# Attention and two feed-forward layers on one core: token blocks by batch, with the short tails gathered in the last block

## The chip, the cores and the metric

The kernel runs on one core of a Trainium2 chip. The metric is the device time of one execution in microseconds (us). Before the change it is 985.03 us, the median of three runs (984.52 to 985.04). Everything is computed in one launch; the host only rearranges inputs.

The engines are named as the profile names them: PE is TensorE (PEld its weight loads), DVE is VectorE, ACT is ScalarE, POOL is GpSimd, SP is SyncE, which issues most of the DMAs.

## The reference

Four batches of 8 heads, 576 queries and keys each, head size 64; then 2304 tokens of width 512 go through two feed-forward layers:

```
scores = q k^T / 8, plus min(-(cum[query] - cum[key]), 0), causal mask
attn   = softmax(scores);   x = attn v                 # [4 * 576, 8 * 64] = [2304, 512]
x      = ((x w_a) * (x w_b)) w_out                     # inner width 1536
h      = x w_in;  g = max(h, 0) + alpha * min(h, 0)    # inner width 2048
out    = g w_out2
```

`cum` is the running sum of max(s, 0) along a head's 576 positions.

## The kernel before

**Tokens.** PE works on blocks of tokens: three of 512 and a last one of 768 (`sizes`, L417). A block is a stretch of 512 or 768 *consecutive* tokens of the 2304, so its borders do not fall on those of the batches, which have 576 tokens. Block 1, for example, holds the last 64 tokens of batch 0 and the first 448 of batch 1. The inputs of the feed-forward layers lie in `xh` and `xl` (two buffers each, 512 tokens, used by the blocks in turn) and, for what is over, in `ovh` and `ovl` (256 tokens). Each number is held as a rounded part (`h`) and a rest (`l`), and each product is made of three matmuls (`mm3`, L1247).

**Attention.** A batch's 576 queries are worked on in two parts: the first 512 (four row tiles of 128, r = 0 to 3), and the last 64, which the text calls the *tail* of the batch (r = 4). For a pair of heads `hp` (four pairs to a batch) the steps are: `loads` (queries and keys `kq`, running sums `cb`, values `v`), `biases` (the bias and mask into a tile `z`), the scores (`s01`, `s23` for the first 512; `s4` for the tail), softmax on DVE and ACT (`soften`), a turn of the probabilities by DVE blocks (`zt`) and through DRAM (`zd`, then read back into `pt` or, for the tail, into the single buffer `pb`), and the product with the values (`av` for the first 512, `av_b` for the tail; `two_av` does both, the tail's first). What leaves `av` is split into `xh` and `xl`; `pieces` (L421) says which part of it goes to which block's tiles, so that the product of batch 1 is split in two pieces (448 and 64 tokens) and that of batch 2 too (384 and 128).

**What runs when.** Batch 0's first 512 queries are done before any feed-forward work (`first_attention`). The rest is a list of steps for each block (`plan`, made by `attention`), which PE takes up between the matmuls of that block: while block 0 is computed, the tail of batch 0 and the first 512 of batch 1; while block 1 is, the tail of batch 1 and the first 512 of batch 2; while block 2 is, the tail of batch 2, batch 3's first 512, and batch 3's tail. A list may begin with a `lead`, put at the end of the list before it (L1919); that of block 0 is issued within `first_attention`, as are its first six steps. Empty steps (`SPACE`) keep a distance before the last product; in block 2 five of them are filled with the first steps of the tail of batch 3, and the other 14 stand behind (L1900).

**What sets the order.** The order of all instructions on each engine is written out when the kernel is built. PE's order follows the loops; that of DVE, ACT, POOL and SP comes from a small model of the engines (`Order`), in which each chain of operations asks for an engine, and the one that could start first gets it; some operations choose between two engines there. `due` takes the next step when its share of the block is reached; `possible` (L1259) may put off scores and `two_av` until their inputs are there by the model; for `av_b` alone it does not look. Each engine then executes its list in order: an instruction that waits holds all behind it.

**Last block.** Block 3 (`ffn_seven`) has no attention beside it. It needs the first 512 tokens and all 256 in `ovh` and `ovl`. At its end `out_2` makes six tiles of 128 tokens of the result, and `store` and `leave` send each to DRAM with one DMA. At the start of blocks 1 and 2 the tokens in `ovh` and `ovl` are copied into the next block's `xh` and `xl` (L1921 to L1924).

Of the kernel before, what the change touches and what calls it, by code (L numbers as in the profile page):

```python
# [21 lines left out]
P = 128  # L22
# [189 lines left out]
def attention_two_moe_kernel(  # L212
# [10 lines left out]
    nc = tc.nc  # L223
# [194 lines left out]
    blocks = [(sum(sizes[:i]), n) for i, n in enumerate(sizes)]  # L418
    NB = len(blocks)

    def pieces(t0, n, blk):  # L421

        b0 = blocks[blk][0]
        k = max(0, min(n, b0 + 512 - t0))
        if k:
            yield 0, k, xh[blk % 2], xl[blk % 2], t0 - b0
        if k < n:
            yield k, n - k, ovh, ovl, t0 + k - b0 - 512
# [357 lines left out]
    def av(b, hp, blk):  # L786
# [25 lines left out]
        run.pe(4 * 1280 / 2.4)  # L812
        run.give(of_vb)
        x_done[blk].append(read_by(at, finish(pv, b * S, QA, hp, blk)))

    def finish(pv, t0, n, hp, blk):
        for o, k, dh, dl, c in pieces(t0, n, blk):
            yield from split(pv[:, o:o + k], dh[:, hp, c:c + k], dl[:, hp, c:c + k], False)
# [28 lines left out]
    def av_b(b, hp, blk):  # L847
# [18 lines left out]
        for c in range(0 if turned else 5):  # L866
# [9 lines left out]
        x_done[min(blk, NB - 1)].append(  # L876
            read_by(at, finish(pv, b * S + QA, QB, hp, min(blk, NB - 1)))
        )

    def two_av(a, b, hp, blk):  # L880

        av_b(b, hp, blk)
        av(a, hp, blk)
# [3 lines left out]
    def first_attention():  # L887
# [12 lines left out]
        for i in range(HP + 2):  # L900
# [8 lines left out]
            if 0 <= i - 2:  # L909
                av(0, i - 2, 0)  # L910
# [21 lines left out]
    def attention(blk):  # L932

        b, a = blk - 1, blk
        has_a = a < B
# [18 lines left out]
        if has_a:  # L954
            lead.append((both, (a, 0, (0, 1))))
        if not has_a or a >= TURN:
            lead.append((biases, (b, 0, (4,))))
        for i in range(HP + 1):
            j = i - 1

            def turns(c):
                for k in range(2 if a < TURN else 0):
                    add(turn, j, a, 2 * j + k, c)

            def last(p, k):
                if blk < TURN:
                    add(t4, p, b, p, k)

            if has_a and a >= TURN:
                add(s4, i, b, i)  # L970
                add(s01, i, a, i)
                add(loads, i + 1, i + 1)
                if blk > 1:
                    add(biases, i + 1, b, i + 1, (4,))
# [7 lines left out]
                if blk == 1:  # L982
                    add(biases, i + 1, b, i + 1, (4,))
                add(both, i + 1, a, i + 1, (0, 1))
            elif has_a:
                add(s01, i, a, i)
                add(both, i, a, i, (2,))
                turns(0)
                add(both, i, a, i, (3,))
                add(s23, i, a, i, 2)  # L990
                last(j, 0)
                turns(1)
                last(j, 1)
                add(s23, i, a, i, 3)
                add(biases, i, b, i, (4,))
                add(loads, i + 1, i + 1)
                turns(2)
                add(both, i + 1, a, i + 1, (0, 1))
                add(two_av, j, a, b, j, blk)
                add(s4, i, b, i)  # L1000
            else:
                add(loads, i + 1, i + 1)
                add(s4, i, b, i)
                add(biases, i + 1, b, i + 1, (4,))
                last(i, 0)
                last(i, 1)
                if i == HP:
                    steps.extend([(lambda: None, ())] * TAIL)
                add(av_b, i - (blk >= TURN), b, i - (blk >= TURN), blk)
# [249 lines left out]
    def possible(f, args):  # L1259
# [5 lines left out]
        if f == two_av:  # L1265
            a, b, hp, _ = args
# [33 lines left out]
    H2 = blocks[-1][1] // 2  # L1300
# [143 lines left out]
    def ffn_seven(blk, sums):  # L1444
        t0, T = blocks[blk]
# [227 lines left out]
        def leave(t, o):  # L1673
            yield from dma(out[t0 + t * P:t0 + (t + 1) * P, :], o)
            run.give(of_t, run.t)

        def store(t):
# [3 lines left out]
            run.spawn(leave(t, o), run.t)  # L1681
# [44 lines left out]
        def out_2(f):  # L1726
# [4 lines left out]
            for t in range(T // P):  # L1731
# [8 lines left out]
                if t == T // P - 1:  # L1740
# [41 lines left out]
    def ffn(blk):  # L1782
        t0, T = blocks[blk]
# [56 lines left out]
        def store(t):  # L1840
# [3 lines left out]
            run.spawn(leave(t, o), run.t)  # L1844

        def leave(t, o):
            yield from dma(out[t0 + t * P:t0 + (t + 1) * P, :], o)
            run.give(of_t, run.t)
# [60 lines left out]
    for blk in range(NB):  # L1909
# [5 lines left out]
        T = blocks[blk][1]  # L1915
# [79 lines left out]
```

## Time and profile before

| | us |
|---|---|
| median of three runs | 985.03 |
| the profiled execution: span from first to last instruction | 982.3 |
| PE busy in it | 963.1 (98%) |
| DVE busy | 748.5 (76%) |
| ACT busy | 558.7 (57%) |
| POOL busy | 223.7 (23%) |
| median less span | 2.7 |

The page gives the profiled execution no time but its span; what the runs have over it, 2.7 us, is taken to lie around it. The page shows PE busy in nine tenths or more of every slice of a fortieth of the span except the first two. The matmuls are pipelined, so a busy PE need not be at its peak: beside the share, the waits of PE are to be read, and how far apart matmuls start.

By the lines of the trace, block 0's matmuls begin at 58 us, block 1's at 276, block 2's at 489 and block 3's at 709.

### The profile page before, as it was taken

What the parts mean: (1) busy time and instruction counts of PE and PEld (TensorE: products, weight loads), DVE (VectorE), ACT (ScalarE), POOL (GpSimd) and SP (SyncE); (2) the same over time, 40 slices, a digit from 0 to 9 for tenths busy, and PEclk for the clock granted to TensorE, in tenths of its full rate; (3) what the DMA queues carried; (4) which work ended last, traced back from release to release, by engine and by line L of the source; (5) the groups of instructions that cost most, each with busy time, mean ns of one, the idle gap of its engine ahead of it and who ended that gap; (6) DMA issues with size and microseconds to landing.
All of it is one profiled execution on the core that took longest, in us unless ns stands there. A gap on an engine that the chain in (4) does not pass through costs nothing.

```text
span 982.3 us, 15862 instructions
## 1 busy us (share of the span) xinstructions
PE 963.1 (98%) x5235; PEld 810.3 (82%) x5235; DVE 748.5 (76%) x1743; ACT 558.7 (57%) x1173; POOL 223.7 (23%) x290
## 2 busy tenths in 40 slices
PE   6989999999999999999999999999999999999998
PEld 5557787778888878888888888888899999999997
DVE  7777886986878788888478868666497888787782
ACT  6856675775855555665455547544552333476453
POOL 2131110431124234563135434522100000000000
PEclk9999999999999999999999999999999999999999
DMA  7589999899788979688388785855402212112101
GB/s 181 185 262 320 347 332 322 293 323 329 245 271 259 304 245 312 194 257 293 112 270 260 218 264 194 251 172 183 165 22 94 78 66 87 43 47 82 61 5 65
DMA packets 140083, 196.78 MB, mean 200 GB/s; under 512 B 35744, under 2 KB 79776, under 8 KB 140000
## 3 DMA queue, kind: packets, MB, share of 16 engines
q1 hardware_dynamic: 130208, 177.93, 58.0%
q10 hardware_dynamic: 9792, 17.83, 4.9%
q8 instruction: 41, 0.67, 0.3%
q14 instruction: 42, 0.34, 0.1%
HBM read 152.13 MB, written 43.59 MB: 199 GB/s over the span
## 4 chain that ended last, share of the span: by engine, by line
PE 84%; DMA 8%; DVE 5%; issue 1%; ACT 1%; SPq 0%; POOL 0%; ACTq 0%; DVEq 0%
PE bank L1248 18%; PE bank L1249 18%; PE bank L1250 18%; PE bank L1886 5%; PE bank L1888 4%; PE bank L1887 4%; DMA cb<-cum_d 3%; PE bank L1735 2%; PE bank L1734 2%; PE bank L1736 2%; PE bank L801 2%; DMA raw<-in_w_dram 2%; PE bank L563 2%; PE bank L544 1%; PE bank L741 1%
## 5 line engine op out<-in xcount | busy, mean ns | idle before, releaser
L1248 PE MATMUL bank<-xh,wh 128*128 128x512 f32 (+1 forms) x620 | 237.9, 384 | 2.0 <-DVE g L292 2.0
L1250 PE MATMUL bank<-xh,wl 128*128 128x512 f32 (+1 forms) x620 | 234.0, 377 | 0.0
L1249 PE MATMUL bank<-xl,wh 128*128 128x512 f32 (+1 forms) x620 | 234.0, 377 | 0.0
L284 ACT ACTIVATE wh<-raw 128x512 fp32r<-128x512 f32 (+1 forms) x198 | 115.1, 592 | 84.4 <-PE bank L1249 35.0
L1248 PEld LDWEIGHTS bank<-xh,wh 128*128 128x128 f32 x620 | 116.4, 188 | 26.1 <-issue 4.6
L1250 PEld LDWEIGHTS bank<-xh,wl 128*128 128x128 f32 x620 | 116.4, 188 | 19.3
L1249 PEld LDWEIGHTS bank<-xl,wh 128*128 128x128 f32 x620 | 116.4, 188 | 18.6
L301 POOL TENSOR_TENSOR wl<-raw,wh 128x512 fp32r<-128x512 f32 x69 | 91.5, 1329 | 110.9 <-ACT wh L284 71.1
L301 DVE TENSOR_TENSOR wl<-raw,wh 128x512 fp32r<-128x512 f32 (+1 forms) x135 | 84.6, 640 | 33.7 <-ACT wh L284 27.8
L276 ACT ACTIVATE z<-z,mn 128x512 f32<-128x512 f32 (+4 forms) x144 | 82.8, 577 | 47.3 <-DVE mn L292 45.9
L1248 PE MATMUL bank<-gh,wh 128*128 128x512 f32 (+1 forms) x240 | 89.5, 373 | 0.0
L1249 PE MATMUL bank<-gl,wh 128*128 128x512 f32 (+1 forms) x240 | 88.7, 370 | 0.4 <-DVE gl L301 0.2
L1250 PE MATMUL bank<-gh,wl 128*128 128x512 f32 (+1 forms) x240 | 88.5, 369 | 0.0
L284 ACT ACTIVATE gh<-g 128x512 fp32r<-128x512 f32 x84 | 52.8, 629 | 43.5 <-DVE g L292 40.1
L1886 PE MATMUL bank<-wh,gh 128*128 128x512 f32 x192 | 76.4, 398 | 0.0
L1029 ACT ACTIVATE top<-raw 128x512 f16<-128x512 bf16 x90 | 68.5, 784 | 12.3 <-DMA raw<-in_w_dram 10.9
L1888 PE MATMUL bank<-wh,gl 128*128 128x512 f32 x192 | 74.8, 389 | 0.0
L1887 PE MATMUL bank<-wl,gh 128*128 128x512 f32 x192 | 74.8, 389 | 0.0
L301 DVE TENSOR_TENSOR gl<-g,gh 128x512 fp32r<-128x512 f32 x69 | 51.6, 748 | 18.8 <-ACT gh L284 18.0
L292 DVE STREAM_TRANSPOSE zt<-z 128x384 f32<-128x384 f32 (+2 forms) x88 | 55.7, 648 | 2.4 <-DMA zd<-zt 1.4
L616 POOL TENSOR_SCALAR_AFFINE_SELECT z<-z 64x64 f32<-64x64 f32 (+2 forms) x80 | 34.0, 432 | 97.3 <-DVE z L606 63.7
L311 DVE TENSOR_SCALAR z<-z,sm 128x512 f32<-128x512 f32 (+4 forms) x100 | 55.0, 573 | 1.3
(151 smaller groups left out, 1918.1 us busy)
## 6 DMA issues: line engine op xcount, KB each, us to landing
raw<-w_d SPq DMA_DIRECT2D x91, 512.0 KB, 4.3
raw<-in_w_dram SPq DMA_DIRECT2D x90, 512.0 KB, 5.6
w_d<-w ACTq DMA_DIRECT2D x46, 256.0 KB, 5.0
zd<-zt SPq DMA_DIRECT2D x48, 192.0 KB, 5.0
pt<-zd SPq DMA_DIRECT2D x48, 192.0 KB, 4.9
kq<-in_kq_a_dram SPq DMA_DIRECT2D x16, 512.0 KB, 5.7
vb<-in_v_dram SPq DMA_DIRECT2D x112, 64.0 KB, 4.4
zd<-zt SPq DMA_DIRECT2D x24, 256.0 KB, 4.0
```

The lines of the kernel that those rows point to most:

```text
L276: nc.scalar.activation(o, i, func, **k)
L284: nc.scalar.activation(o, i, AF.Copy, scale=by)
L292: f(*args, **k)
L301: (nc.gpsimd if eng == "pool" else nc.vector).tensor_tensor(o, i0, i1, op=ALU.subtract)
L311: (nc.gpsimd if eng == "pool" else nc.vector).tensor_scalar(o, i, s0, s1, op0=ALU.mult, op1=ALU.mult)
L1029: nc.scalar.activation(top.bitcast(F16).rearrange("p (n t) -> p n t", t=2)[:, :, 1], r.bitcast(BF16)[:, 4:4 + 4 * WN].rearrange("p (n t) - ...
L1248: nc.tensor.matmul(o, wh, ih, start=first, stop=False)
L1249: nc.tensor.matmul(o, wh, il, start=False, stop=False)
L1250: nc.tensor.matmul(o, wl, ih, start=False, stop=last)
L1886: nc.tensor.matmul(acc[t], gh[:, c], wh, start=first, stop=False)
L1887: nc.tensor.matmul(acc[t], gh[:, c], wl, start=False, stop=False)
L1888: nc.tensor.matmul(acc[t], gl[:, c], wh, start=False, stop=last)
```

## The change

The three blocks of 512 now are the first 512 queries of batches 0, 1 and 2; the last block of 768 holds the first 512 of batch 3 and then the four tails of 64. So nothing that a block before the last needs comes from a tail. `pieces` and `finish` are gone (each product is split in one piece), and so are the copies at the start of blocks 1 and 2. While block 0 is computed there is now the first 512 of batch 1 alone; the tail of batch 0 is appended to the steps of block 1, in the same way in which batch 3's is appended in block 2. `leave` sends a tile of the tails as two DMAs of 64 rows, since its two halves belong to two batches, and `out_2` of the last block makes the two tail tiles first. The branch for batches below `TURN` goes with it; since `TURN` is 1 and only batch 0's first 512 are below it, it was not used.

```diff
     sizes = [512] * (NT // 512 - 1) + [512 + NT % 512]
-    blocks = [(sum(sizes[:i]), n) for i, n in enumerate(sizes)]
-    NB = len(blocks)
-    def pieces(t0, n, blk):
...
+    NB = len(sizes)
+
+    def leave(b, t, o):
+        if t < QA // P:
+            yield from dma(out[b * S + t * P:b * S + (t + 1) * P, :], o)
+        else:
+            ends = [(2 * t - 2 * QA // P + j + 1) * S for j in range(2)]
+            halves = [
+                run.spawn(dma(out[e - QB:e, :], o[j * QB:(j + 1) * QB]), run.t)
+                for j, e in enumerate(ends)
+            ]
...
-        x_done[blk].append(read_by(at, finish(pv, b * S, QA, hp, blk)))
+        parts = (x[b % 2][:, hp, :] for x in (xh, xl))
+        x_done[b].append(read_by(at, split(pv, *parts, False)))
...
-        x_done[min(blk, NB - 1)].append(
-            read_by(at, finish(pv, b * S + QA, QB, hp, min(blk, NB - 1)))
-        )
+        parts = (x[:, hp, b * QB:(b + 1) * QB] for x in (ovh, ovl))
+        x_done[NB - 1].append(read_by(at, split(pv, *parts, False)))
...
-    def attention(blk):
-        b, a = blk - 1, blk
-        has_a = a < B
+    def attention(a, b):
...
         def loads(i):
-            if has_a:
+            if a is not None:
                 load_kq(a, i, 0)
...
-            load_kq(b, i, 1)
-            load_sums(b, i, 1)
-            load_v(b, i, 1)
+            if b is not None:
+                load_kq(b, i, 1)
+                load_sums(b, i, 1)
+                load_v(b, i, 1)
+
+        def tail(f, pair, *args):
+            if b is not None:
+                add(f, pair, b, *args)
...
-                add(two_av, j, a, b, j, blk)
+                if b is None:
+                    add(av, j, a, j)
+                else:
+                    add(two_av, j, a, b, j)
...
-            for t in range(T // P):
+            tiles = [*range(QA // P, T // P), *range(QA // P)]
+            for t in tiles:
...
-    plan = [attention(blk) for blk in range(1, NB)] + [([], [])]
-    last, more = attention(NB)
-    tail = last + more
-    plan[NB - 2][1][:] = [
-        tail.pop(0) if not args else (f, args) for f, args in plan[NB - 2][1]
-    ] + tail
+    plan = [attention(b + 1, b or None) for b in range(NB - 1)] + [([], [])]
+    for blk, b in ((1, 0), (NB - 2, NB - 1)):
+        last, more = attention(None, b)
+        tail = last + more
+        plan[blk][1][:] = [
+            tail.pop(0) if not args else (f, args) for f, args in plan[blk][1]
+        ] + tail
...
-        if 1 <= blk < NB - 1:
-            n = max(0, blk * S + QA - blocks[blk + 1][0])
-            nc.vector.tensor_copy(xh[(blk + 1) % 2][:, :, 0:n], f32(ovh[:, :, 0:n]))
-            nc.vector.tensor_copy(xl[(blk + 1) % 2][:, :, 0:n], f32(ovl[:, :, 0:n]))
```

The first place where the order moves is SP's queue just ahead of block 0. `kq_a` holds queries and keys of the first 512 (two DMAs to a pair, one for each head), `kq_b` and `cb` are those of a tail, `vb` are values, `raw` are encoded weights. Before:

```order
L317 DMA raw<-in_w_dram 128x2048
L317 DMA kq<-in_kq_a_dram 64x1024
L317 DMA kq<-in_kq_b_dram 128x704
L317 DMA cb_564<-cum_d 64x576
L317 DMA vb<-in_v_dram 32x4x128 x2
L317 DMA raw<-in_w_dram 128x2048 x2
L317 DMA kq<-in_kq_a_dram 64x1024
L317 DMA cb_564<-cum_d 64x576
```

After:

```order
L317 DMA raw<-in_w_dram 128x2048
L317 DMA kq<-in_kq_a_dram 64x1024
L317 DMA vb<-in_v_dram 32x4x128
L317 DMA raw<-in_w_dram 128x2048 x2
L317 DMA kq<-in_kq_a_dram 64x1024
L317 DMA vb<-in_v_dram 32x4x128 x2
```

Ahead of the second half of batch 1's first `kq_a` there are now one `kq_b`, one `cb` and one `vb` fewer.

The second place is DVE's list when the scores of that pair arrive, just ahead of block 0. `z<-cb` is the bias of the tail of batch 0, the rows with 288 elements read its scores, those with 128 the first scores of batch 1. Before:

```order
L301 TENSOR_TENSOR xl_109<-bank_103,xh_107 128x512
L606 TENSOR_SCALAR z<-cb_564,cumq 128x576
L288 CAST wh<-w_523 128x512
L301 TENSOR_TENSOR wl<-w_523,wh 128x512
L292 ISA z,mn<-bank_102,z 128x288
L292 ISA mn 128x1
L292 ISA z,mn<-bank_103,z 128x288
L292 ISA mn 128x1
L292 ISA z,mn<-bank_104,mask 128x128
```

After:

```order
L301 TENSOR_TENSOR xl_109<-bank_103,xh_107 128x512
L288 CAST wh<-w_523 128x512
L301 TENSOR_TENSOR wl<-w_523,wh 128x512
L292 ISA z,mn<-bank_102,mask 128x128
L292 ISA mn 128x1
L292 ISA z,mn<-bank_103,mask 128x128
```

The bias, which waits for `cb`, and the two reads of the tail's scores no longer stand ahead of batch 1's first scores, which now lie in banks 102 and 103 in place of 104 and 105.

The third place is DVE's list ahead of the first gate of block 0 (`g`, the product that frees the second of the two banks into which PE multiplies). Before:

```order
L292 STREAM_TRANSPOSE zt<-z 128x384 x3
L292 ISA z,mn<-bank_99,mask 128x512
L292 ISA mn 128x1
L292 ISA z,mn<-bank_100,mask 128x512
L292 ISA mn 128x1
L292 SCALAR_TENSOR_TENSOR w_652<-raw,top_148 128x512
L292 TENSOR_SCALAR sm<-sm 128x1
L292 SCALAR_TENSOR_TENSOR w_700<-raw,top_149 128x512
L292 RECIPROCAL sm<-sm 128x1
L292 TENSOR_SCALAR sm<-sm 128x1
L311 TENSOR_SCALAR z<-z,sm 128x512
L292 TENSOR_TENSOR g<-bank_102,a_sb 128x512
```

After:

```order
L292 STREAM_TRANSPOSE zt<-z 128x384 x3
L292 RECIPROCAL sm<-sm 128x1
L292 TENSOR_SCALAR sm<-sm 128x1
L292 SCALAR_TENSOR_TENSOR w_641<-raw,top_149 128x512
L311 TENSOR_SCALAR z<-z,sm 128x512
L292 SCALAR_TENSOR_TENSOR w_648<-raw,top_148 128x512
L292 STREAM_TRANSPOSE zt<-z 128x512
L301 TENSOR_TENSOR wl<-w_641,wh 128x512
L292 TENSOR_TENSOR g<-bank_102,a_sb 128x512
```

The two reads of 512 scores have moved further ahead, and a turn of 512 (`zt`) and a weight's rest (`wl`) now stand between the turns of 384 and the gate.

## Rows read from the trace of the kernel before

**Rows 1.** Waits of PE from 0 to 983 us: us in total, times, longest.
```profile
PE bank L563 <- DMA kq<-in_kq_a_dram: 3.1, 2, 2.6
PE bank L1248 <- DVE g L292: 2.0, 1, 2.0
...
PE bank L544 <- DVE ovl L301: 0.8, 1, 0.8
```

**Rows 2.** Windows of blocks 1 and 2: length, busy PE, PEld, DVE, ACT, POOL, clock, DMA, GB/s.
```profile
276.00:489.00 213.00, 212.08 (x1135) 175.75 (x1134) 166.32 (x381) 121.46 (x254) 84.46 (x99) 1.00 0.79 250
489.00:709.00 220.00, 220.00 (x1234) 181.78 (x1233) 155.44 (x388) 117.87 (x252) 84.72 (x110) 1.00 0.71 218
```

**Rows 3.** Windows of 4 us around the start of block 0.
```profile
48.00:52.00 4.00, 1.77 (x11) 1.06 (x9) 0.38 (x1) 2.84 (x7) 0.00 (x0) 1.00 1.06 313
52.00:56.00 4.00, 3.64 (x14) 1.68 (x16) 2.88 (x13) 0.00 (x0) 1.02 (x2) 0.58 0.81 226
...
68.00:72.00 4.00, 1.97 (x9) 1.32 (x8) 4.00 (x13) 3.27 (x9) 1.72 (x4) 1.00 0.94 320
```

**Rows 4.** Timeline of PE, with the wait before an instruction in brackets.
```profile
33.97 2.38 PE L808 MATMUL bank<-pt,vb 128*64 128x512 f32 x16
...
48.11 1.14 PE L741 MATMUL bank<-kq 128*128 128x288 f32 x4
...
52.36 0.37 PE L563 MATMUL bank<-kq 64*128 64x128 f32 x1 [2.60 <-DMA kq<-in_kq_a_dram]
...
53.93 3.40 PE L808 MATMUL bank<-pt,vb 128*64 128x512 f32 x16
...
70.61 0.50 PE L1248 MATMUL bank<-xh,wh 128*128 128x512 f32 x1 [2.04 <-DVE g L292]
```

**Rows 5.** Timeline of DVE from the wait for `cb` to the gate.
```profile
53.08 0.52 DVE L606 TENSOR_SCALAR z<-cb,cumq 128x576 f32<-128x576 f32 x1 [4.71 <-DMA cb<-cum_d]
...
55.33 0.28 DVE L292 CUSTOM_DVE_ANT_0 z<-bank,mask 128x128 f32<-128x128 f32 x1
...
59.42 0.83 DVE L292 STREAM_TRANSPOSE zt<-z 128x640 f32<-128x640 f32 x1
...
66.25 0.58 DVE L292 STREAM_TRANSPOSE zt<-z 128x384 f32<-128x384 f32 x1 [1.39 <-DMA zd<-zt]
...
69.88 0.67 DVE L292 TENSOR_TENSOR g<-bank,a_sb 128x512 f32<-128x512 f32 x1
```

**Rows 6.** Timeline of PE in block 2: a `two_av`, and an `av_b` alone.
```profile
642.45 0.80 PE L862 MATMUL bank<-pb,vb 128*64 128x64 f32 x20
643.08 2.36 PE L801 MATMUL bank<-pt,vb 128*64 128x128 f32 x40
645.37 0.50 PE L1886 MATMUL bank<-wh,gh 128*128 128x512 f32 x1
...
659.52 0.80 PE L862 MATMUL bank<-pb,vb 128*64 128x64 f32 x20
660.25 0.50 PE L1886 MATMUL bank<-wh,gh 128*128 128x512 f32 x1
```

**Rows 7.** Timeline of PE in block 2: the scores of two pairs of tails.
```profile
490.23 1.13 PE L741 MATMUL bank<-kq 128*128 128x288 f32 x4
...
666.51 1.13 PE L741 MATMUL bank<-kq 128*128 128x288 f32 x4
```

**Rows 8.** Timeline of SP: reads into `pb`, in block 2.
```profile
504.55 0.37 SPq L317 DMA_DIRECT2D pb<-zd  x1
...
674.71 0.42 SPq L317 DMA_DIRECT2D pb<-zd  x1
```

**Rows 9.** The tile `pb`: us from issue of its 16 reads to landing.
```profile
DMA to landing us min/median/max: 3.5/4.3/7.3
```

**Rows 10.** Timeline of ACT at the end: copies of the six result tiles.
```profile
975.18 4.08 ACT L284 ACTIVATE o<-bank 128x512 f32<-128x512 f32 x6 [5.21 <-PE bank L1736]
```

**Rows 11.** Timeline of SP at the end: the DMAs of these tiles.
```profile
975.80 3.81 SPq L317 DMA_DIRECT2D out_dram<-o  x6
```

More of the change, by code (lines that the diff above doesn't have):

```diff
@@ L417, in attention_two_moe_kernel @@
     sizes = [512] * (NT // 512 - 1) + [512 + NT % 512]
-    blocks = [(sum(sizes[:i]), n) for i, n in enumerate(sizes)]
-    NB = len(blocks)
-    def pieces(t0, n, blk):
[L423 to L428, printed above, removed]
+    NB = len(sizes)
[8 more added lines that the diff above has]
+            ]
+            for half in halves:
+                yield half
+        run.give(of_t, run.t)
     pb_t, scores = {}, []
@@ L784, in settle, with av @@
             run.need(e_t.pop(key))
-    def av(b, hp, blk):
+    def av(b, hp):
         turned = b >= TURN
@@ L813, in av @@
         run.give(of_vb)
-        x_done[blk].append(read_by(at, finish(pv, b * S, QA, hp, blk)))
-    def finish(pv, t0, n, hp, blk):
-        for o, k, dh, dl, c in pieces(t0, n, blk):
-            yield from split(pv[:, o:o + k], dh[:, hp, c:c + k], dl[:, hp, c:c + k], False)
+        parts = (x[b % 2][:, hp, :] for x in (xh, xl))
+        x_done[b].append(read_by(at, split(pv, *parts, False)))
     def t4(b, hp, j):
@@ L845, in t4, with av_b @@
         e_t[b, hp, 4 + j] = read_by(at, chain())
-    def av_b(b, hp, blk):
+    def av_b(b, hp):
         turned = b + 1 >= TURN
@@ L875, in av_b, with two_av @@
         run.give(of_pb)
-        x_done[min(blk, NB - 1)].append(
-            read_by(at, finish(pv, b * S + QA, QB, hp, min(blk, NB - 1)))
-        )
-    def two_av(a, b, hp, blk):
-        av_b(b, hp, blk)
-        av(a, hp, blk)
+        parts = (x[:, hp, b * QB:(b + 1) * QB] for x in (ovh, ovl))
+        x_done[NB - 1].append(read_by(at, split(pv, *parts, False)))
+    def two_av(a, b, hp):
+        av_b(b, hp)
+        av(a, hp)
     HP = H // 2
@@ L909, in first_attention @@
             if 0 <= i - 2:
-                av(0, i - 2, 0)
+                av(0, i - 2)
             if i < HP:
@@ L948, in loads @@
                 load_v(a, i, 0)
-            load_kq(b, i, 1)
-            load_sums(b, i, 1)
-            load_v(b, i, 1)
+            if b is not None:
[5 more added lines that the diff above has]
+                add(f, pair, b, *args)
         lead = [(loads, (0,))]
-        if has_a:
+        if a is not None:
             lead.append((both, (a, 0, (0, 1))))
-        if not has_a or a >= TURN:
+        if b is not None:
             lead.append((biases, (b, 0, (4,))))
@@ L959, in attention @@
             j = i - 1
[L961 to L970, printed above, removed]
+            if a is not None:
+                tail(s4, i, i)
                 add(s01, i, a, i)
                 add(loads, i + 1, i + 1)
-                if blk > 1:
-                    add(biases, i + 1, b, i + 1, (4,))
+                tail(biases, i + 1, i + 1, (4,))
                 add(both, i, a, i, (2,))
@@ L979, in attention @@
                     steps.extend([(lambda: None, ())] * SPACE)
-                add(two_av, j, a, b, j, blk)
+                if b is None:
+                    add(av, j, a, j)
+                else:
+                    add(two_av, j, a, b, j)
                 add(s23, i, a, i, 3)
-                if blk == 1:
-                    add(biases, i + 1, b, i + 1, (4,))
                 add(both, i + 1, a, i + 1, (0, 1))
[L985 to L1000, printed above, removed]
             else:
                 add(loads, i + 1, i + 1)
[L1003 to L1006, printed above, removed]
+                tail(s4, i, i)
+                tail(biases, i + 1, i + 1, (4,))
                 if i == HP:
                     steps.extend([(lambda: None, ())] * TAIL)
-                add(av_b, i - (blk >= TURN), b, i - (blk >= TURN), blk)
+                tail(av_b, j, j)
         return lead, steps
@@ L1265, in possible @@
         if f == two_av:
-            a, b, hp, _ = args
+            a, b, hp = args
             keys = [(a, 2 * hp + j, r) for j in range(2) for r in (0, 2, 3)] + [(b, hp, 4)]
@@ L1299, in attention_two_moe_kernel @@
     t_hl, pools = [], {}
-    H2 = blocks[-1][1] // 2
+    H2 = sizes[-1] // 2
     acc2 = [banks[d // 2][:, d % 2 * 256:d % 2 * 256 + 256] for d in range(KD)]
@@ L1444, in ffn_seven @@
     def ffn_seven(blk, sums):
-        t0, T = blocks[blk]
+        T = sizes[blk]
         lo, hi = slice(0, H2), slice(H2, T)
@@ L1671, in rectified @@
             return end
-        def leave(t, o):
-            yield from dma(out[t0 + t * P:t0 + (t + 1) * P, :], o)
-            run.give(of_t, run.t)
         def store(t):
@@ L1680, in store @@
             yield from copy(o, (acc + banks[0:2])[t], 1.04, SHRUNK ** 2)
[L1681 removed]
+            run.spawn(leave(blk, t, o), run.t)
         def x2_part(o, j, d, c):
@@ L1739, in out_2 @@
                     o_done[t] = run.spawn(store(t))
-                if t == T // P - 1:
+                if t == tiles[-1]:
                     run.give(of_w)
@@ L1782, in ffn @@
     def ffn(blk):
-        t0, T = blocks[blk]
+        T = sizes[blk]
         xhb, xlb = xh[blk % 2], xl[blk % 2]
@@ L1843, in store @@
             yield from copy(o, acc[t], 1.04, SHRUNK ** 2)
[L1844 to L1848, printed above, removed]
+            run.spawn(leave(blk, t, o), run.t)
         for f in range(NF1 + 1):
@@ L1914, in attention_two_moe_kernel @@
         run.landing = LANDING[1]
-        T = blocks[blk][1]
+        T = sizes[blk]
         while x_done[blk]:
```

## The prediction

> **What bounds the kernel now.** I first read what PE waits for over the whole execution [rows 1]. The reader is to see how little it is: 3.1 us on `kq_a` (2.6 of it in one piece), 2.0 us on a gate `g`, 0.8 us on a split into `ovl`; what else stands in that view is the very start and short waits of batch 0's first products, which the change doesn't touch, and a wait of 0.2 us. So PE is the bound from block 0 on, and a change that leaves the matmuls as they are can win only what PE loses around 48 to 71 us, and a little at 353 us.
>
> Next come the windows of 4 us there [rows 3]. From 48 to 52 us PE is busy for 1.77 of 4 us while DVE does 0.38 us of work and the DMA engines are full (share 1.06, 313 GB/s); from 52 to 56 us PE's granted clock is 0.58, so most of that stretch ran at 1.2 GHz in place of 2.4; from 68 to 72 us PE is busy for half the time and DVE for all of it. The timelines name the instructions. PE does the scores of the tail of batch 0 (48.11), then waits 2.60 us until 52.36 for the second half of batch 1's first `kq_a`; the sixteen value products that follow take 3.40 us, where sixteen like them took 2.38; at 70.61 it has waited 2.04 us for the gate [rows 4]. DVE stood for 4.71 us for `cb`, the running sums of that tail, until 53.08, everything else behind it, and reached the gate at 69.88 [rows 5]. Blocks 1 and 2 are the other picture: PE is busy 212.08 of 213 and 220.00 of 220 us, with DVE at 166 and 155 [rows 2].
>
> **What the change does, part by part.** The matmuls are the same in number and shape before and after; they are only moved.
>
> *The start (A).* One `kq_b` (128x704), one `cb` (64x576) and one `vb` (32x4x128, all four bytes each) no longer stand ahead of the second half of `kq_a`: 573 KB, at 313 GB/s [rows 3] 1.8 us. PE then goes on at 52.4 - 1.8 = 50.5. Its wait begins a little earlier than before, since the tail's scores (1.1 us from 48.11) are gone: it is still some 2.0 us long, not 2.6. From 52.36 to the end of the wait on the gate less that wait is 70.61 - 2.04 - 52.36 = 16.2 us of work. Off this go 1.0 us for the value products at full clock (3.40 - 2.38) and some 0.4 for the scores beside them, and 0.3 since the last scores of that pair now stand ahead of block 0 and not between its matmuls; added is the first score step of batch 1's second pair, which the order now has ahead of the gate (1.3 us, an estimate from the 1.57 us from 52.36 to 53.93, three quarters of such a step at half clock). PE reaches the gate at 50.5 + 16.2 - 1.7 + 1.3 = 66.3.
>
> DVE: from its first read of batch 1's scores (55.33) to the gate (69.88) it took 14.55 us [rows 5]. Between them go the tail's scaling and turn (0.52, as its bias of the same 576 columns took, and 0.83, with 0.3 of small ones) and one decode of weights (0.6); a turn of 512 columns and a weight's rest come in (0.7 and 0.6): 13.6 us. It starts at about 50.5 in place of 55.33, since neither the wait for `cb` nor two reads of the tail's scores stand ahead: the gate begins at 64.1 and is done at 64.8. But the additional turn needs one of three `zt` buffers back from its write to DRAM, as the one at 66.25 did for 1.39 us: 0 to 2 us later, so 64.8 to 66.8. PE goes on at 66.3 to 66.8; I take 66.5. That is 4.1 us ahead of 70.61, with 1.3 us of work done early and 1.1 us (the tail's scores) left for later: A = -4.3. Bounds: everything at fault gone (2.6 + 2.0 + 1.4 + 0.3) -6.3; a DVE that comes 1.7 us later than I have it, -2.6.
>
> The clock in this sum: after the 2.60 us of wait the granted clock fell, after the 2.04 us it stayed at 1.00 [rows 3, 4]; the wait I expect is nearer to the second. [...]
>
> *Tail products by themselves (B).* In `two_av` the tail's product stands just ahead of that of the batch, 642.45 to 645.37 = 2.92 us to the next feed-forward matmul; alone it takes 0.73 us (659.52 to 660.25), and the other part of `two_av` 2.29 us (643.08 to 645.37): 0.1 more for the two apart, and an entry and an exit more among matmuls of another shape, an estimate of 0.2 from the same rows [rows 6]. That is 0.3 us for each of the four pairs of batch 0's tail. By the order after, the non-feed-forward pieces in PE's row rise from 66 to 69; one product stands right behind scores and saves its entry. B = +1.0 (0.8 to 1.3). The scores cost the same wherever they stand.
>
> *Copies and pieces (C).* The casts `xh<-ovh` and `xl<-ovl` and the second pieces of the splits are work of DVE and ACT that PE doesn't wait for, except 0.8 us on `ovl` [rows 1]. That piece is gone; a like wait may stand elsewhere: -0.4 (-0.8 to 0).
>
> *Block 1 (D).* It gets 14 more steps, with five in the empty places: 56, as many as block 2 has before, and there PE waits for nothing [rows 2]. But block 1 has 166 us of DVE in 213 us against 155 in 220, and decodes weights still. Tail 0 adds some 12 us to DVE (four pairs, 3 us each, by the rows above), with 9 us of PE: 178 of 222 us, 80%. Of `av_b` the planner asks nothing ahead: it may be issued while its `pb` is still on its way. By the order after, the first pair's scores and its `av_b` are apart by 48 feed-forward matmuls, 0.23 us each (a third of what a tile's copy takes at the end [rows 10]), and a `two_av`: 1 + 11 + 3 = 15 us; the second pair's by 14.5. In block 2 the chain took 674.71 - 666.51 = 8.2 us to the read's issue and 3.5 to 7.3 us from there [rows 7 to 9]: 11.7 to 15.5 us. So waits of 0 to 1 us each; with denser steps D = +0.8 (0 to 3).
>
> *The end (E).* Six copies in 4.08 us, six stores in 3.81 [rows 10, 11]; the two tail tiles now are four stores. An issue on SP takes 0.37 to 0.42 us [rows 8], two of them about as long as the 0.68 from copy to copy, and what they fall behind with two tiles is made up with the four that follow: 0 (to +0.4).
>
> Sum: -4.3 + 1.0 - 0.4 + 0.8 + 0 = -2.9. The span would go from 982.3 to 979.4, and with the 2.7 us around it the median from 985.03 to 982.1. The bounds together: -6.3 + 0.8 - 0.8 = -6.3, so 978.7; -2.6 + 1.3 + 0 + 3 + 0.4 = +2.1, so 987.1.
>
> **Rivals.** *The gate takes the place of the load (no change).* PE is ahead, but DVE is not: its list, with a turn of 512 columns ahead of the gate, waits for buffers, and the gate comes at 68.2: A = -2.6, and with D at 1.2 the sum is -0.8: 984.2. For it: DVE has no idle time from 68 to 72 us, and its wait at 66.25 was of this kind. Against: it begins its list 4.8 us earlier, with less in it.
>
> *Tail 0 is late in block 1 (slower).* The first pair of a tail in block 2 took 504.55 - 490.23 = 14.3 us to the issue of its read, since SP had other work ahead, and up to 7.3 us from there: 21.6 us. With such chains at the end of block 1, the first pair's `av_b` waits 6.6 us, the second's hardly more (its chain runs meanwhile), the last pair's, which is apart by 17 us, 4.7. In place of D's 0.8 that is 11.3: +7.6, so 992.6. It decides from waits of 2.9 + 0.8 + 2.0 = 5.7 us on. For it: `av_b` isn't put off. Against: at the end of block 1 the engines had little to do, and in block 2 none of the tails' products was waited for [rows 2].
>
> *All of the start's loss goes.* Neither the load nor the gate holds PE: A = -6.3, sum -4.9: 980.1.
>
> **Chances.** A time counts as changed from 0.2% on, about what a measurement of this kernel tells from none: 2.0 us, so faster means under 983.06. The forecast (-2.9, its own range 981 to 983.5) has 0.45, all of the loss gone 0.15, the gate in its place or D eating the gain 0.27, the late tail 0.13. A quarter of the forecast's cases lie above 983.06 or near it, and I put 0.04 of them with no change: faster 0.56, no change 0.31, slower 0.13. The range of 8 in 10 runs from 979.0 to 987.0, to the bounds of the sum, with most of the late tail left out.
>
> **What would show it.** DVE has no wait on `cb` ahead of block 0; PE's wait on `kq_a` is about 2 us long and ends near 50.5; the clock stays at 1.00 from 52 to 56 us; the first matmul after the gate stands near 66.5. PE has at most 2 us of waits in block 1, all near `av_b` or batch 2's scores; block 1 is some 9 us longer than before and block 0 as much shorter; the last matmul's distance to the end is the same. The forecast is wrong if the gate's matmul comes after 68.2, or if waits in front of `av_b` add up to more than 3 us.

## The result, and the profile after

The changed kernel takes 991.91 us (median of four runs, 990.33 to 992.84) against 985.03 (four runs, 984.52 to 986.05): 1.0064 times as long, with an interval of 1.0047 to 1.0081. It is slower by 6.9 us, where 982.1 was forecast and the range ended at 987.0. The profiled execution took 991.26 us; its span of 989.5 us is 7.2 longer than the 982.3 of before. Of the later runs of the kernel before, one took 1068.49 us at a lower granted clock (0.851); the ratios further down leave it out. L566, L744, L804, L811 and L1223 are what were L563, L741, L801, L808 and L1248.

| term of the sum | forecast, us | in the trace, us |
|---|---|---|
| A, the start up to the gate | -4.3 | -6.9 |
| B and C, products by themselves, copies | +0.6 | +0.6 (what is left) |
| D, tail 0 in block 1 | +0.8 | +10.9 (8.2 of waiting, 2.7 at half clock) |
| E, the end | 0 | +2.6 |
| sum | -2.9 | +7.2 |

The right column compares one execution of each kernel; how it comes out of the views is told with each of them. The first is again what PE waits for over the whole execution; it answers to [rows 1].

```profile
PE bank L862 <- DMA vb<-in_v_dram: 7.9, 1, 7.9
...
PE bank L566 <- DMA kq<-in_kq_a_dram: 1.1, 2, 0.7
PE bank L1224 <- DVE xl L292: 0.9, 1, 0.9
```

The waits on the gate and on `ovl` are gone, that on `kq_a` is down from 3.1 to 1.1 us, and a single new one of 7.9 us is more than all of these: the values `vb` in front of an `av_b` (L862). PE's timeline at the start (start, length, instruction, wait ahead of it) answers to [rows 4]:

```profile
33.26 2.38 PE L811 MATMUL bank<-pt,vb 128*64 128x512 f32 x16
...
48.97 0.37 PE L566 MATMUL bank<-kq 64*128 64x128 f32 x1 [0.75 <-DMA kq<-in_kq_a_dram]
...
49.94 2.37 PE L811 MATMUL bank<-pt,vb 128*64 128x512 f32 x16
...
54.34 0.50 PE L1223 MATMUL bank<-xh,wh 128*128 128x512 f32 x1
...
63.94 0.39 PE L1223 MATMUL bank<-xh,wh 128*128 128x512 f32 x1
```

The last of these rows is the matmul that waited 2.04 us for the gate at 70.61 (the 37th of block 0 in both kernels). It stands 6.7 us earlier and waits for nothing. PE has done 1.3 us of work early by then (the second pair's scores) and left 1.1 us for later (the tail's): A = -6.9. Not all of this is the change: the sixteen value products of the first row, which stand ahead of every place where PE's order moves, begin 0.7 us earlier too (33.26 against 33.97). The value products at 49.94 take 2.37 us, as at full clock. DVE's timeline shows why the gate is no wait; it answers to [rows 5]:

```profile
49.83 0.29 DVE L292 CUSTOM_DVE_ANT_0 z<-bank,mask 128x128 f32<-128x128 f32 x1 [1.09 <-PE bank L566]
...
61.53 0.71 DVE L292 STREAM_TRANSPOSE zt<-z 128x512 f32<-128x512 f32 x1 [0.22 <-DMA zd<-zt]
...
62.74 0.68 DVE L292 TENSOR_TENSOR g<-bank,a_sb 128x512 f32<-128x512 f32 x1
```

It reads the scores 5.5 us earlier than before, the wait for a `zt` buffer is 0.22 us, and `g` is done at 63.42.

Then the loss. The windows by block (length, busy PE, PEld, DVE, ACT, POOL, granted clock, DMA share, GB/s) answer to [rows 2]; their bounds are where the blocks now begin and end:

```profile
54.00:263.00 209.00, 208.06 (x1049) 165.77 (x1048) 164.66 (x344) 142.66 (x265) 44.63 (x41) 1.00 0.87 297
263.00:494.00 231.00, 223.13 (x1234) 183.75 (x1233) 175.73 (x412) 128.71 (x268) 93.89 (x117) 0.98 0.83 259
494.00:714.00 220.00, 220.00 (x1234) 181.77 (x1233) 156.09 (x385) 116.37 (x247) 82.80 (x109) 1.00 0.73 219
```

Block 1 is 18 us longer, where the prediction had some 9 for the work of tail 0, and for 7.9 us of it PE stands; block 2 is as before. The timeline of PE in block 1 has the place:

```profile
410.63 1.13 PE L744 MATMUL bank<-kq 128*128 128x288 f32 x4
...
425.66 1.13 PE L744 MATMUL bank<-kq 128*128 128x288 f32 x4
434.66 1.33 PE L862 MATMUL bank<-pb,vb 128*64 128x64 f32 x20 [7.87 <-DMA vb<-in_v_dram]
435.93 0.80 PE L1854 MATMUL bank<-wh,gh 128*128 128x512 f32 x1
436.52 0.63 PE L1855 MATMUL bank<-wl,gh 128*128 128x512 f32 x1
...
440.68 0.39 PE L1225 MATMUL bank<-xh,wl 128*128 128x512 f32 x1
440.90 0.40 PE L1223 MATMUL bank<-xh,wh 128*128 128x512 f32 x1
```

It is the first `av_b` of tail 0. It stands right behind the scores of the second pair. Less these scores (0.76 us from their start to the next matmul's, as e1 below shows them followed by work) PE loses 434.66 - 425.66 - 0.76 = 8.2 us. What follows is slow: the product takes 1.27 us to the next matmul where 0.73 is usual [rows 6], and the twelve matmuls from 435.93 to 440.90 take 4.97 us where, by the spacing of such matmuls elsewhere in the trace, 2.85 would do (0.227 each, 0.13 more for the first). That is 2.7 us more, and the windows of 4 us there name the reason in the column before the last two, the granted clock:

```profile
428.00:432.00 4.00, 0.00 (x0) 0.00 (x0) 3.56 (x10) 1.88 (x4) 0.15 (x1) 0.79 0.54 141
...
436.00:440.00 4.00, 4.00 (x10) 3.14 (x11) 0.23 (x1) 0.23 (x1) 0.00 (x0) 0.50 0.70 227
440.00:444.00 4.00, 4.00 (x18) 3.26 (x17) 0.88 (x2) 1.45 (x3) 0.00 (x0) 0.93 0.77 238
```

It fell from 2.4 to 1.2 GHz while PE stood, and came back near 440 us. Why the values were late is seen on SP, which issues the loads in a fixed order:

```profile
400.96 3.03 SPq L317 DMA_DIRECT2D vb<-in_v_dram  x2
...
419.83 0.33 SPq L317 DMA_DIRECT2D zd<-zt  x1
...
424.12 0.58 SPq L317 DMA_DIRECT2D pb<-zd  x1
424.79 2.47 SPq L317 DMA_DIRECT2D vb<-in_v_dram  x4
431.54 0.33 SPq L317 DMA_DIRECT2D zd<-zt  x1
431.90 1.90 SPq L317 DMA_DIRECT2D vb<-in_v_dram  x3
```

A `vb` of a tail is six loads, and `load_v` has the planner issue each when it takes the one before to have landed. The first pair's first one is issued at 401, its last at 432, and ahead of that last one stands the `zd` write of the *second* pair, whose probabilities exist only after the scores at 425.66. The chain of waits runs through exactly this:

```profile
430.67 0.85 DVE zt L292
...
431.54 0.33 SPq L317
431.86 0.04 issue
431.90 0.60 SPq L317
...
432.55 2.13 DMA vb<-in_v_dram
434.68 1.32 PE bank L862 x20
```

At the end, the timelines of ACT and SP answer to [rows 10, 11]:

```profile
979.76 2.66 ACT L284 ACTIVATE o<-bank 128x512 f32<-128x512 f32 x4 [5.22 <-PE bank L1708]
983.45 0.60 ACT L284 ACTIVATE o<-bank 128x512 f32<-128x512 f32 x1 [1.03 <-DMA out_dram<-o]
984.78 0.60 ACT L284 ACTIVATE o<-bank 128x512 f32<-128x512 f32 x1 [0.74 <-DMA out_dram<-o]
```
```profile
980.38 5.35 SPq L317 DMA_DIRECT2D out_dram<-o  x8
```

Two of the six copies now wait for a store, and SP has eight issues. The last matmul starts at 982.77, 6.7 us before the end of the span; before it was 982.3 - 978.19 = 4.1. E = +2.6 in this execution; in other executions with the same end it is less, as the part on the end shows. The remainder of the sum, 7.2 + 6.9 - 10.9 - 2.6 = 0.6, is put down to B and C, which no view shows by themselves.

### The profile page after: what moved, and what is told of

Same layout as the page of the kernel before. It is cut to its first block, busy times and chain, and to the rows that moved or that the text cites. A ratio compares the mean times of both kernels' runs of the same rounds, so it can differ in the third digit from the quotient of the medians.

```text
span 989.5 us, 15862 instructions
## 1 busy us (share of the span) xinstructions
PE 964.1 (97%) x5235; PEld 811.8 (82%) x5235; DVE 745.3 (75%) x1725; ACT 559.3 (57%) x1162; POOL 231.9 (23%) x291
## 4 chain that ended last, share of the span: by engine, by line
PE 94%; DVE 2%; DMA 2%; ACT 2%; issue 0%; SPq 0%; ACTq 0%
PE bank L1223 21%; PE bank L1224 21%; PE bank L1225 21%; PE bank L1854 5%; PE bank L1856 4%; PE bank L1855 4%; PE bank L804 3%; PE bank L1707 2%; PE bank L1706 2%; PE bank L1708 2%; PE bank L547 2%; PE bank L744 1%; PE bank L566 1%; PE bank L862 1%; DMA kq<-in_kq_a_dram 1%; ACT z L276 1%
## 5 line engine op out<-in xcount | busy, mean ns | idle before, releaser
L1223 PE MATMUL bank<-xh,wh 128*128 128x512 f32 (+1 forms) x620 | 237.8, 384 | 0.0
L1223 PEld LDWEIGHTS bank<-xh,wh 128*128 128x128 f32 x620 | 116.5, 188 | 25.7 <-issue 6.5
L1223 PE MATMUL bank<-gh,wh 128*128 128x512 f32 (+1 forms) x240 | 89.6, 373 | 0.0
L301 POOL TENSOR_TENSOR wl<-w,wh 128x512 fp32r<-128x512 f32 x24 | 31.8, 1323 | 134.8 <-ACT wh L284 92.0
L311 DVE TENSOR_SCALAR z<-z,sm 128x512 f32<-128x512 f32 (+4 forms) x103 | 59.0, 597 | 1.3
```

The source lines that it names most:

```text
L301: (nc.gpsimd if eng == "pool" else nc.vector).tensor_tensor(o, i0, i1, op=ALU.subtract)
L311: (nc.gpsimd if eng == "pool" else nc.vector).tensor_scalar(o, i, s0, s1, op0=ALU.mult, op1=ALU.mult)
L1223: nc.tensor.matmul(o, wh, ih, start=first, stop=False)
```

## The experiments

The theory (T1): three separate things, the start's gain by the move of tail 0, one late product with the half clock that it leaves behind, and an end that is longer by half stores and their buffers. Against it: T2, block 1 is too dense and what is put off is waited for later; T2', the chain of the probabilities would have been as late as the values; T3, the gain at the start comes with the token blocks; and for single places T4 to T7, named where they belong. e1 to e4, e5 to e8, and e9 each have their own runs of the kernel before, on the same chip as theirs (a different one for each of the three groups, so times are best compared through the ratios).

| run | median, us (runs) | before, us | ratio, 95% interval |
|---|---|---|---|
| e1 av_b put off | 981.65 (12) | 984.58 | 0.9972 (0.9960 to 0.9985) |
| e2 first values early | 989.09 (6) | 984.58 | 1.0055 (1.0033 to 1.0077) |
| e3 tail 0 in block 0 | 992.00 (6) | 984.58 | 1.0099 (1.0068 to 1.0131) |
| e4 buffers for the end | 991.16 (6) | 984.58 | 1.0070 (1.0052 to 1.0087) |
| e5 as e3, order of before | 986.59 (12) | 984.76 | 1.0021 (1.0006 to 1.0036) |
| e6 e1 and e4 | 980.28 (6) | 984.76 | 0.9954 (0.9936 to 0.9972) |
| e7 e6, one store a tail tile | 989.36 (7) | 984.76 | 1.0041 (1.0023 to 1.0058) |
| e8 tail tiles last | 990.72 (6) | 984.76 | 1.0058 (1.0040 to 1.0076) |
| e9 e6, tail tiles last, two store queues | 980.47 (8) | 984.67 | 0.9954 (0.9937 to 0.9971) |

**e1: put the late product off.**

```
-        rings = 1 if f == two_av else 2
-        if f not in (s01, s23, s4, two_av):
+        rings = 1 if f in (two_av, av_b) else 2
+        if f not in (s01, s23, s4, two_av, av_b):
             return True
...
+        if f == av_b:
+            k = b, hp, 4
+            return k in e_t and seen(e_t[k], v_t[b, hp, 1][1])
```

> The planner asks of av_b what it asks of two_av (probabilities turned and back, values landed, a free bank) before it issues it; otherwise the changed kernel. T1 (one wait, then half clock): the loss of the change is the 8.15 us that PE stood in front of the first av_b of tail 0 and the 3.0 us that the matmuls behind it took longer at 1.2 GHz. By the order that av_b now stands 51 feed-forward matmuls (11.6 us) after the second pair's scores instead of right behind them, later than the 434.6 us at which its values landed: both go, 991.9 - 11.2 = 980.7, no PE wait over 1 us from 400 to 490 us, granted clock 1.00 there. T2 (block 1 is too dense: the work of tail 0 does not fit, and what is put off is waited for later): a wait of 4 us or more comes back before the end of block 1, and the time stays above 987.

Measured 981.65, 10.3 us less than the changed kernel. PE's timeline has work behind the scores, and the product 12 us later without a wait; the window is at full clock:

```profile
427.19 1.13 PE L744 MATMUL bank<-kq 128*128 128x288 f32 x4
427.95 0.61 PE L1857 MATMUL bank<-wh,gh 128*128 128x512 f32 x1
...
439.86 0.80 PE L862 MATMUL bank<-pb,vb 128*64 128x64 f32 x20
```
```profile
432.00:436.00 4.00, 4.00 (x19) 3.30 (x19) 3.87 (x8) 1.70 (x4) 1.67 (x2) 1.00 0.56 187
```

No wait comes back in block 1. T2 falls: the block has room for tail 0, and the loss was this one place.

**e2: only the values early.**

```
...
+                if (b, hp, u) == (0, 0, 1):
+                    for c in [run.spawn(p, run.t, SL_QK) for p in parts]:
+                        yield c
+                    return
...
```

> The six loads of vb of the first pair of tail 0 are planned side by side instead of one after the other's landing, so that they stand on SP ahead of the pb read and of the second pair's zd write; PE's order is that of the changed kernel. T1 in its narrow form (SP's order alone made the values late): PE then waits only for pb, which landed at 429.35 where PE stood from 426.15: a wait of 3.2 us instead of 8.15, 4.9 us less, and of the 3.0 us at half clock none to all goes: 984 to 987. T2' (the probabilities' chain would have been as late anyway, the values only came last in the records): the wait stays over 6 us, with pb named as what ended it, and the time at 990 to 992.

Measured 989.09, between the two. The wait is shorter by 2.8 us, not by 4.9, and the clock falls all the same:

```profile
425.18 1.13 PE L753 MATMUL bank<-kq 128*128 128x288 f32 x4
431.34 1.33 PE L871 MATMUL bank<-pb,vb 128*64 128x64 f32 x20 [5.03 <-DVE zt L292]
```
```profile
424.66 0.54 SPq L317 DMA_DIRECT2D pb<-zd  x1
```
```profile
DMA to landing us min/median/max: 6.6/6.6/6.6
```

DVE's transposition, which the wait names, was done at 421.2; what came last is the read into `pb` (SP's timeline, then the landing in the view of that tile): 424.66 + 6.6 = 431.3. So both inputs were late. The chain from the first pair's scores (410.14 here) to their `pb` takes 21.1 us and alone makes PE wait 5.0 us; the values add 2.8 to it. In the changed kernel's own trace this chain was 2.1 us shorter (the read issued at 424.12 landed in 5.5 us, at 429.6): there it would by itself have made PE wait 3.2 us, and the values add 5.0. Either way T1 in its narrow form and T2' each have a part of it.

**e3 and e5: the token blocks without the move.** In e3 tail 0 goes back to block 0; in e5 the steps there are in the order of before as well.

```
-    plan = [attention(b + 1, b or None) for b in range(NB - 1)] + [([], [])]
-    for blk, b in ((1, 0), (NB - 2, NB - 1)):
+    plan = [attention(b + 1, b) for b in range(NB - 1)] + [([], [])]
+    for blk, b in ((NB - 2, NB - 1),):
```

> The new token blocks and the half stores, but tail 0 stays spread over block 0, as in the kernel before (its loads stand in the lead of block 0 again). T1: the gain of 6.9 us at the start belongs to the move of tail 0: PE's waits of 2 to 3 us on kq_a and about 2 us on the gate are back, no wait in front of tail 0's products, the 0.96 us on ovl stays away, and the end is 2.6 us longer: 985.0 - 1.0 + 2.6 = 986.6 (985.5 to 987.5). T3 (the gain at the start comes with the token blocks, whose splits have no second pieces): the waits at the start stay short, and the time is 979 to 982.

e3 took 992.0 (991.2 to 999.4) and met neither number. Its view of PE's waits has the start as before (3.4 us on `kq_a`), against T3, but new waits as well:

```profile
PE bank L1223 <- ACT a_sb L284: 3.8, 1, 3.8
PE bank L566 <- DMA kq<-in_kq_a_dram: 3.4, 2, 2.9
PE bank L547 <- DVE xl L301: 2.1, 1, 2.1
```

e5's edit, beside e3's, is `biases` of tail 0 behind `s23` in the list again. With it the wait on `a_sb` is gone and that on `xl` is 0.2 us, so e3's own order of steps had made them.

> As e3 (new token blocks and half stores, tail 0 spread over block 0), but with the steps of block 0 in the order of the kernel before, so that PE's list of matmuls is word for word the one before. T1 (the start's gain belongs to the move, e3 was slow by its own order of steps): e3's waits of 4.0 us on a_sb at 161 us and of 3.3 us at 358 us go, the waits on kq_a (2 to 3 us) and on the gate (about 2 us) are there as before, the 0.96 us on ovl is not, the end is 2.6 us longer: 1.6 us over the kernel before, 986.2 (985.2 to 987.5). T3 (the token blocks give the gain at the start): 3 to 6 us under the kernel before. T5 (the token blocks themselves cost something in block 0): more than 3 us over the kernel before.

986.59, as T1 has it. The load and the half clock behind it are there as in the kernel before (PE's timeline, and the window at 52 us); the wait on the gate is 0.66 us and not about 2, as PE comes to it later (its value products took 4.43 us, in the kernel before 3.40) and the gate itself a little earlier:

```profile
51.80 0.58 PE L566 MATMUL bank<-kq 64*128 64x128 f32 x1 [2.93 <-DMA kq<-in_kq_a_dram]
```
```profile
52.00:56.00 4.00, 4.00 (x16) 1.71 (x18) 3.45 (x17) 0.56 (x1) 1.02 (x2) 0.50 0.83 233
```

T3 falls: the token blocks with their half stores cost 1.8 us (0.6 to 3.5 by the interval), and the start's gain belongs to the move. T5, which wanted more than 3 us, is not borne out.

**e4, e8, e7 and e9: the end.** e4 gives the tail tiles output buffers of their own, e8 undoes the order of the tiles.

```
-            yield of_t
-            o = ft.tile([P, DM], F32, name="o", tag="t")
+            if t < QA // P:
+                yield of_t
+                o = ft.tile([P, DM], F32, name="o", tag="t")
+            else:
+                o = pools["big"]([P, DM], F32, "o", 2)
```
```
-            tiles = [*range(QA // P, T // P), *range(QA // P)]
+            tiles = [*range(T // P)]
```

> The last block's two tail tiles take output buffers of their own (two more, in space that is free in that block), so that none of the six copies waits for a store; otherwise the changed kernel. T1: the copies at the end waited 1.03 and 0.74 us for stores of the tail tiles, whose buffers come back only when both halves are out. Without it the last copy is done at about 983.9 and its store issued by 984.3 instead of 985.17: 0.9 to 1.4 us less, 990.5 to 991.0. T4 (the end is bound by SP, which needs 0.56 to 0.61 us for a half store and has eight stores to issue): the last store is not issued earlier than now, and the time stays at 991.9.

> The changed kernel with the last block's tiles in the order 0 to 5, the two tail tiles last instead of first. T1 (the tail-first order costs by the buffers that come back late): the last copy is not waited for, the four half stores are the last on SP, the last one issued 5.2 us behind the first copy instead of 5.4, landing 2.35 us later: 0.5 to 1.0 us less than the changed kernel, 991.0 to 991.4. T7 (tail-first is what keeps four half stores off the very end): 0.6 to 1.2 us more, 992.5 to 993.1.

e4: the copies run without a wait, SP is done with its last issue 2.2 us behind the start of the last matmul in place of 3.0, and the span ends 990.1 - 984.19 = 5.9 us behind it in place of 6.7:

```profile
981.18 4.03 ACT L284 ACTIVATE o<-bank 128x512 f32<-128x512 f32 x6 [5.21 <-PE bank L1711]
```
```profile
981.80 4.60 SPq L317 DMA_DIRECT2D out_dram<-o  x8
```

The 0.8 us at the very end are no more than the spread of this distance. e1 has the end of the changed kernel, waits for stores included, and the row of its last matmul, with a span of 979.4 us, gives 5.7:

```profile
973.71 0.39 PE L1711 MATMUL bank<-wh,gl 128*128 128x512 f32 x1
```

So for each profile, in us behind the start of its last matmul (from the timelines of PE, SP and, for e9, ACT, and the span):

| run | last issue of a store is done | span ends |
|---|---|---|
| before | 1.4 | 4.1 |
| changed | 3.0 | 6.7 |
| e1, same end | 3.0 | 5.7 |
| e2, same end | 3.0 | 5.8 |
| e5, same end | 3.0 | 6.4 |
| e8, tail tiles last | 2.9 | 5.8 |
| e4, buffers | 2.2 | 5.9 |
| e6, buffers | 2.2 | 5.8 |
| e9, buffers, tail tiles last, two queues | 1.9 | 5.2 |

From the last issue to the end it takes 2.7 to 3.8 us, even with one and the same end. The buffers bring the last issue forward, which is against T4; that they bring the end forward is not shown, neither by these distances nor by the time of e4 (991.16). e8's time, 990.72, is a little under what T1 gave and well under T7's 992.5: T7 falls. That tail-first costs something is not shown either, since e8's 5.8 is also the distance of e1 and e2. What is left in e4, 1.8 us over before, lies for 0.8 us ahead of the last issue's end and for 1.0 behind it. e7 is e6 with each tail tile stored at once:

```
-            halves = [
-                run.spawn(dma(out[e - QB:e, :], o[j * QB:(j + 1) * QB]), run.t)
...
+            both_ends = out.rearrange("(b s) d -> b s d", s=S)[k:k + 2, QA:S, :]
+            yield from dma(both_ends, o)
```

> e6, and each tail tile goes out in one store of 2x64x512 instead of two halves. T1 (what is left of the longer end is SP's time for eight issues, of which the halves took 0.56 to 0.61 us each): six issues, two of them at about 0.6 us, follow the copies as before, the last store is issued some 0.2 us behind the last copy, and the end comes back to 4.0 to 4.6 us behind the last matmul: 1.2 to 1.8 us less than e6, 979.1 to 979.7. T6 (a store that is spread over two places takes its time in the queue, not in the issue): the end stays over 5.4 us, and the time within 0.5 us of e6.

It is 9 us slower than e6 and fits neither. Six issues take SP 7.38 us, and the window behind the last matmul shows the DMA engines all but idle:

```profile
970.66 7.38 SPq L317 DMA_DIRECT2D out_dram<-o  x6
```
```profile
972.00:976.00 4.00, 1.43 (x7) 0.84 (x5) 0.00 (x0) 1.80 (x4) 0.00 (x0) 1.00 0.13 35
```

A share of 0.13 is about two of sixteen engines. So e7 says nothing of T6. e9 asks again, as e6 with the tail tiles last and the second half of each issued by ACT:

```
+            def half_by_act(e, i):
+                yield {"act": 330}, 700
+                nc.scalar.dma_start(out[e - QB:e, :], i)
...
```

> e6 with the two tail tiles last, and of each the second half stored from ACT's queue instead of SP's. In e6 the distance from the start of the last matmul to the end of the span is 978.2 - 972.39 = 5.8 us, in the kernel before 4.1. T1 (what is left of the longer end is SP's time for eight issues, the last at 4.6 us behind the first copy): two issues fewer on SP, the last ones of either queue by some 4.7 us, but only of 64 rows: a distance of 5.2 to 5.5 us. T6 (it is the transfer: 64 rows land later than 128 rows, whoever issues them): 5.7 us or more. In the time this is 0 to 0.6 us below e6's 980.3, less than can be told; the profile decides.

The distance is 981.6 - 976.42 = 5.2 us, where T1 put it. But it is one profile, 0.6 us below e6's, and profiles with one and the same end are up to 1.0 apart, so T1 is supported here and not shown. The time is e6's, as expected. Of the 1.1 us that e9's end is still over that of before, 0.6 lie behind the last issue (3.3 us from there to the end, where before had 2.7); why stays open.

**e6: both mends.**

> e1 and e4 together: av_b put off, and output buffers of their own for the two tail tiles. T1: the two have nothing in common, so 981.65 - 0.8 = 980.9 (980.0 to 981.6), no PE wait over 1 us after the start but the one on xl at 167 us, and the end 5.8 us behind the last matmul in place of 6.6. T4 (eight issues on SP bound the end with or without the buffers): no faster than e1, 981.6.

980.28: 4.5 us faster than the kernel before, some 11.6 than the changed one. With the late product put off, the change is worth 0.3% (e1), and 0.5% with the buffers as well; the two intervals overlap, so what the buffers add is not shown.

## Why the prediction was wrong

*D failed, and with it the sign.* The prediction said of block 1 that "of `av_b` the planner asks nothing ahead: it may be issued while its `pb` is still on its way", set 15 us between scores and product against a chain of 11.7 to 15.5, and came to "waits of 0 to 1 us each". Two things were wrong in that. The chain was taken from one pair of block 2, 8.2 us from the scores to the read's issue; here these are 13.5 us (410.63 to 424.12), and with the landing it took 19.0 us in the changed kernel and 21.1 in e2. The rival of a late tail had 21.6 and put the first product's wait at 6.6; by itself the chain makes 3.2 (changed kernel) to 5.0 (e2). And the product has a second input: `vb` was never followed to its new place, though `load_v` is among the moved steps: its six loads on SP are counted nowhere there. It came last, and the wait was 8.2.

*The half clock was priced at the start and forgotten here.* 2.7 of D's 10.9 us are a consequence of the wait; a rival that adds up waits alone comes out short. That rival's 992.6 is near the 991.9 measured, but by luck: it has two waits of 6.6 and 4.7 us, there was one, and the clock, and A and E were off as well.

*The planner did not ask, and could have told.* e1 adds nothing but the question, and the same model then puts the product off by 12 us. So by its own times something that the product needs was not there yet when the changed kernel issued it; the fault was the missing question, not a wrong time.

*A went the right way, by more.* The second half of `kq_a` was to come 1.8 us earlier, with a wait of 2.0; it came 3.4 earlier (48.97 against 52.36), with 0.75. By SP's timeline the second half is issued 4.47 us behind the first in all eight profiles with this order of the start and 5.39 in the kernel before, so the order gives 0.9 us; 0.7 are the earlier start of this execution; and the landing took 6.1 us from its issue where it took 7.9 before. That landing takes 6.1 to 8.2 us in the eight, so the 1.8 us of bytes at 313 GB/s are not shown by themselves. The eight profiles have longest waits on it of 0.7, 0.9, 0.9, 1.0, 1.0, 1.9, 2.0 and 2.9 us, so the profile of the changed kernel stands at the good end and the forecast's 2.0 within the spread. The 37th matmul of block 0 begins at 63.5 to 65.7 us in seven of them. In e9, with 2.87, the value products begin 3.2 us later (53.12) and take 1.0 longer, and that matmul begins at 68.10: A is -2.7 there. Of the rivals, that all of the start's loss goes was nearest here, and that the gate takes the load's place fell: DVE reached the gate 1.4 us earlier than forecast, and the wait for a buffer was 0.22 us.

*B and C* were forecast at 0.6 together, and 0.6 is left over. That does not show either by itself: as a difference of single executions it holds whatever else moved. Of C, the 0.8 us on `ovl` went and 0.9 us on `xl` came, inside its bounds.

*E failed:* "an issue on SP takes 0.37 to 0.42 us, two of them about as long as the 0.68 from copy to copy" took the length of a half store from other DMAs. A store of 128 rows here took 0.33 us on SP before, the eight of the changed kernel have a median of 0.55; and the tail tiles' buffers, which come back after two stores, were not looked at. By the profiles with this end it is 1.6 to 2.6 us instead of 0: the last issue is done some 1.5 us later than before, and what follows it took up to 1.1 us longer.

That e1 comes out at the forecast's -2.9 us is luck too: in its own trace A is -5.4 (the 37th matmul at 65.45) and E is +1.6.

Of what the prediction wanted to see, no wait on `cb`, the clock at 1.00 from 52 us and an earlier gate came; "waits in front of `av_b` add up to more than 3 us" was its own mark of failure.

## What to carry to other kernels

For a step that is moved, list every input that its instructions wait for, and follow each back to the queue that brings it: the one that was never late in its old place is the one to look at. A wait on PE can be paid twice, in itself and in the matmuls at half clock behind it: here that was so behind the waits of 2.60 to 2.93 us on `kq_a` and of 5.03 and 7.87 us in front of `av_b`, and not behind those of 0.75 to 1.98 us on `kq_a` and of 2.04 us on the gate. Where an order is planned ahead, a step that the planner issues without asking is the first suspect; here one condition turned a loss of 6.9 us into a gain of 2.9.

## What the runs showed of the hardware

The granted clock at the start, by the wait on `kq_a` ahead of it: after waits of 0.75, 1.92 (e1) and 1.98 us (e4) the sixteen value products took 2.37 to 2.38 us, at 2.4 GHz; after 2.60 [rows 4] and 2.87 (e9) they took 3.4, much of it at 1.2, and after 2.93 (e5) 4.43, with a granted clock of 0.50. e9's timeline of PE:

```profile
51.50 0.40 PE L575 MATMUL bank<-kq 64*128 64x128 f32 x1 [2.87 <-DMA kq<-in_kq_a_dram]
...
53.12 3.36 PE L820 MATMUL bank<-pt,vb 128*64 128x512 f32 x16
```

So here one us of a load's landing decided over another us of PE's time. How much of the spread of the runs comes from this is not shown. Nor does the length of one wait alone tell what the clock does: in the kernel before, waits of 1.72 and 1.06 us close together (up to 19.49 and 21.44) went with a granted clock of 0.74 from 20 to 24 us.

e7's stores of a tail tile, 256 KB as 2x64x512, moved at some 35 GB/s where e6's stores of 64x512 and 128x512 kept the DMA engines at a share of 0.98 and 301 GB/s in the same window. The Trainium skill ("DMA: Bandwidth & Descriptors", "Rules for kernel authors") says that the slowest dimension of the access pattern sets over how many of the sixteen engines a transfer is spread; with a leading 2 that is at most two, and the share of 0.13 agrees.
